# Earlier first Gram copies, earlier key loads, and a solve of the inverses with paired neighbours

## The chip, the cores and the metric

The kernel runs on one core of a Trainium2 chip. The metric is the device time of one execution in microseconds (us): 745.49 is the median of three runs of the kernel before, which lie between 743.66 and 747.66. The engines are named as in the profile: PE multiplies matrices (PEld is its loading of weights), DVE is the vector engine, ACT the scalar engine, POOL the general engine, SP the engine that issues most transfers.

## What is computed

Three layers stand one behind the other. The first is a linear attention with the delta rule, over 4 batches of 8 heads, 768 steps and vectors of 48. Its core in the reference:

```
k_n = k / (np.linalg.norm(k, axis=-1, keepdims=True) + 1e-06)
for t in range(S):
    kt, vt, bt = (k_n[:, :, t], v[:, :, t], beta[:, :, t, None])
    y[:, :, t] = np.einsum('bhd,bhde->bhe', q[:, :, t], state)
    v_old = np.einsum('bhde,bhd->bhe', state, kt)
    state = state + bt[:, :, :, None] * np.einsum('bhd,bhe->bhde', kt, vt - v_old)
```

The second takes the 4 x 768 x 384 output x through a product with w_in (384 x 1024), a gelu, a layer norm of one half, a mix over the 768 positions with w_sg, a gate and a product with w_out, and adds x. The third mixes each position with the one before it and forms sigmoid(xr w_r) * (relu(xk w_k)^2 w_v).

## The kernel before

The 768 steps are cut into 12 chunks of 64, two chunks to a group. Within a chunk the recurrence is replaced by a triangular system. For each group g, `gram(g)` lets PE form products of the keys: eight parts (4 parts i with 16 head pairs each in two halves), in blocks of 32 x 32, of which the diagonal blocks go to `GD` and the others to `GL`, by one ACT copy each (L342). `solver(g)` then inverts, on DVE, the 32 x 32 unit triangular matrices of all heads, 32 per partition: it transposes GD into `NT` (L360), forms the norms and c = beta / norm^2 (L364 to L380), scales the four 8 x 8 diagonal blocks of NT by c (L389), inverts the 8 x 8 blocks row by row in `Yt` (i = 1 to 7; each row is a product L355 and a reduce L393), copies the result to `Dm` and `NT` (L401, L403), and joins 8 x 8 blocks to 16 x 16 and to 32 x 32, again with products and reduces that all go through one buffer `tmp`. The last step transposes Dm into `DT` (L440). From the second group on, `couple(g, k)` multiplies GL and DT on PE (L456) to carry one 32-block into the next.

A prelude forms the first group: keys (kT0, kT1) are loaded, `gram(0)` runs in two sets, first the diagonal blocks (columns 0 to 32, four copies, `diag[:4]`), later the others (`diag[4:]`), then the first products of the scan and `gram(1)`. Meanwhile the weights of w_in are loaded and rounded into two parts each by a chain of ACT (L164), four DVE operations (L169 to L175), POOL (L177), ACT (L120) and POOL (L123). `early(n, t)` moves such background work on by n steps of t us.

Then 12 chunks are scanned in two halves of heads. `st_rq`, `st_d`, `st_n`, `st_s` and `st_y` are PE products with ACT copies between them (r at L473, the keys' products at L513, u at L526, the state at L540 and L555). `tick` brings in the background work, the solver of the next group and the Gram products of the one after that. The units of the second layer that are ready fill PE's stream in between. From some 300 us on PE works on the layers two and three alone.

The program order on PE, ACT, DVE and POOL is the order of the Python statements (`manual_schedule`), so what an engine does next is fixed by what was written first, and each engine waits in that order. A list `streams` holds running generators such as the solver; the background step lets each of them issue what its `yield` costs allow.

The order of SP's queue matters in the prelude: beta is written first in the program, then the keys, the weights of w_in, the queries and the tokens.

Of the kernel before, what the change touches and what calls it, by code (L numbers as in the profile page):

```python
# [7 lines left out]
F32 = mybir.dt.float32  # L8
# [3 lines left out]
AF = mybir.ActivationFunctionType  # L12
# [20 lines left out]
LOW0 = 1  # L33
WARM = 4
SV = 60
B0 = 1.0
PRE = 0.8
GRAM0 = 7
# [35 lines left out]
def vw(t, off, dims):  # L74

    a = t[:]
    return bass.AP(a.tensor, a.offset + off, [list(a.ap[0])] + [list(d) for d in dims])
# [9 lines left out]
def fused_kernel(  # L87
# [143 lines left out]
    def slot(tag, shape, dtype=F32):  # L231
        return wq.tile(shape, dtype, name="s" + tag, tag=tag)
# [16 lines left out]
    with ExitStack() as at:  # L249
# [13 lines left out]
        def load_k(s):  # L263
            if s >= 12:
                return
            kT[s] = kTb[s % NKT]
            nc.sync.dma_start(out=kT[s], in_=kt_d[s])

        def load_tok(s):
            t = ap2.tile([P, 2, NPR, D], F32, name="vk")  # L270
            vt[s], kt[s] = t[:, 0], t[:, 1]
            for h in range(2):
                nc.sync.dma_start(out=t[64 * h:64 * h + 64, 0], in_=vk[64 - 64 * h:128 - 64 * h, s, 0])
            nc.sync.dma_start(out=t[:, 1], in_=vk[:, s, 1])
# [3 lines left out]
                r = 64 * (1 - h)  # L278
                nc.sync.dma_start(out=SQ[o][s % 2][h][r:r + D, :, D:], in_=q_d[s, o, h])

        beta_sb = ap1.tile([P, NG, 32], F32, name="beta_sb")
        for h in range(2):
            nc.sync.dma_start(out=beta_sb[64 * h:64 * h + 64], in_=beta[64 - 64 * h:128 - 64 * h])

        banks = [ps2]

        def bank():
# [1 line left out]

        Sps = [ps1.tile([P, 8, D], F32, name=f"sps{o}") for o in range(2)]  # L290
        warm = ap1.tile([P, P], mybir.dt.bfloat16, name="warm")
        load_k(0)
        load_k(1)
        NT, GD, Dm = (slot(x, [P, 32, 32]) for x in G0[:3])
        tmp = slot(G0[3], [P, 1024])
        GLb = [slot(G0[4], [P, NU, 32]), slot(W0[2], [P, NU, 32]),
# [51 lines left out]
        Yt = ap1.tile([P, 16, 16], F32, name="Yt")  # L348
        GDs, GLs, DTs, neTs, joined = {}, {}, {}, {}, set()

        def product(a_off, a_dims, a_t, b_off, b_dims, b_t):

            sh = [d[1] for d in a_dims]
            tv = vw(tmp, 0, [(sh[1] * sh[2], sh[0]), (sh[2], sh[1]), (1, sh[2])])
            V.tensor_tensor(tv, vw(a_t, a_off, a_dims), vw(b_t, b_off, b_dims), op=ALU.mult)  # L355
            return tv, sh[0] * sh[1] * sh[2] / 960 + 0.16

        def solver(g):

            V.transpose(out=NT, in_=GDs[g])  # L360
            G.memset(Yt, 0.0)
            yield 1.14
            ss = ap1.tile([P, 32], F32, name="ss")
            V.tensor_scalar(ss, vw(NT, 0, [(33, 32)]), -1.0, 1e-36, op0=ALU.mult, op1=ALU.max)  # L364
            yield 0.2
            ne = yield from rsqrt(ap1, ss, 32, "rn")
            V.tensor_tensor(ne, ne, ss, op=ALU.mult)
            yield 0.2
            V.tensor_scalar(ne, ne, EPS, None, op0=ALU.add)
            yield 0.2  # L370
            neT = ap2.tile([P, 32], F32, name="neT")
            V.transpose(out=neT, in_=ne)
            neTs[g] = neT
            rn = ap1.tile([P, 32], F32, name="rn")
            V.reciprocal(rn, ne)
            yield 0.4
            V.tensor_tensor(rn, rn, rn, op=ALU.mult)
            yield 0.2
            c = ap1.tile([P, 32], F32, name="c")
            V.tensor_tensor(c, rn, beta_sb[:, g], op=ALU.mult)  # L380
            yield 0.2

            V.tensor_copy(vw(Yt, 0, [(64, 4), (9, 8)]), c.rearrange("p (m i) -> p m i", m=4))
            yield 0.1
            for m in range(4):
                blk = NT[:, 8 * m:8 * m + 8, 8 * m:8 * m + 8]
                V.tensor_tensor(blk, blk, vw(c, 8 * m, [(1, 8), (0, 8)]), op=ALU.mult)  # L389
                yield 0.15  # L390

            def total(o_ap, tv, t):
                V.tensor_reduce(out=o_ap, in_=tv, axis=AX.X, op=ALU.add)  # L393
                return t

            for i in range(1, 8):
                tv, t = product(32 * i, [(264, 4), (0, i), (1, i)], NT,
                                0, [(64, 4), (8, i), (1, i)], Yt)
                yield t
                yield total(vw(Yt, i, [(64, 4), (8, i)]), tv, t)  # L400
            V.tensor_copy(vw(Dm, 0, [(264, 4), (32, 8), (1, 8)]), vw(Yt, 0, [(64, 4), (1, 8), (8, 8)]))  # L401
            yield 0.4
            V.tensor_copy(vw(NT, 16, [(264, 2), (32, 8), (1, 8)]), vw(Yt, 0, [(64, 2), (8, 8), (1, 8)]))  # L403
            yield 0.3
            for dst in (0, 1):
                for p in range(2):
                    o = 16 * p
                    if dst == 0:
                        tv, t = product(32 * (o + 8) + o, [(32, 8), (0, 8), (1, 8)], NT,
                                        128 * p, [(0, 8), (8, 8), (1, 8)], Yt)  # L410
                        ov = vw(NT, 8 + 528 * p, [(1, 8), (32, 8)])
                    else:
                        tv, t = product(33 * (o + 8), [(32, 8), (0, 8), (1, 8)], Dm,
                                        8 + 528 * p, [(0, 8), (32, 8), (1, 8)], NT)
                        ov = vw(Dm, 32 * (o + 8) + o, [(32, 8), (1, 8)])
                    yield t
                    yield total(ov, tv, t)
                    if dst and p == 0:
                        V.tensor_copy(vw(NT, 24, [(1, 8), (32, 8)]), ov)
                        yield 0.2  # L420
            for last in (0, 1):
                if last == 0:
                    ops = [(vw(Yt, 16 * j, [(1, 16), (16, 4)]),
                            (32 * 16 + j, [(32, 16), (0, 4), (1, 16 - j)], NT,
                             16 + 33 * j, [(0, 16), (32, 4), (1, 16 - j)], NT))
                           for j in (12, 8, 4, 0)]
                else:
                    ops = [(vw(Dm, 32 * (16 + i), [(32, 4), (1, 16)]),
                            (32 * (16 + i) + 16, [(32, 4), (0, 16), (1, i + 4)], Dm,
                             0, [(0, 4), (16, 16), (1, i + 4)], Yt)) for i in (0, 4, 8, 12)]  # L430
                for i, (ov, args) in enumerate(ops):
                    tv, t = product(*args)
                    yield t
                    if g == 0 and last and i == 1:
                        V.memset(warm, 0.0)
                    if g == 0 and last and i == 2:
                        scale_v(0)
                    yield total(ov, tv, t)
            DT = DTb[g % 2]
            V.transpose(out=DT.rearrange("p u i -> p i u"), in_=Dm)  # L440
            DTs[g] = DT
            yield 1.14
            if g:
                p = point[0] + LAGC
                p += -p % 6 if p % 6 > 2 else 0
                for k in range(2):
                    later.append((p + 6 * k, lambda k=k: couple(g, k)))
# [16 lines left out]
        def scale_v(s):  # L464
            G.tensor_tensor(vt[s], vt[s], vw(neTs[s // 2], NPR * (s % 2), [(1, NPR), (0, D)]),
                            op=ALU.mult)
# [319 lines left out]
        for o in range(2):  # L786
            load_q(0, o)
        load_tok(0)
        diag = gram(0, ((0, 32), (32, 64)))
        for job in diag[:4]:  # L790
            for _, f in job:
                f()
            early(1, NPRE)
        streams.append([point[0], solver(0), "solve"])
        for s in range(2, NKT):
            load_k(s)
# [38 lines left out]
        def tick():  # L835
            g, n = divmod(point[0], 24)
            point[1] = min(g, 1) + 1
            gg, nn = divmod(point[0] - GRAM0, 24)
            if nn == 0 and 0 <= gg and gg + 2 < NG:
                grams.extend(gram(gg + 2))  # L840
            if n == 0 and g + 1 < NG:
                streams.append([point[0] + SOLVE0, solver(g + 1), "solve"])
            late = point[0] >= LATE
            if point[0] < LASTP and jobs and len(running) < RUN[1 + late] and n % (2 if late else EVERY) == 0:
                start_job(LJ5 if late else LJ)
            background(BUDGET * (B0 if g == 0 else 1))
            while len(jobs) > n_rest and len(running) < RUN[0]:
                start_job()
            if grams and (point[0] - GRAM0) % GSTEP == 0:
                for _, f in grams.pop(0):  # L850
                    f()
                used[0] += 1.1
                dense[0] += 1
            point[0] += 1
# [398 lines left out]
```

## Time and profile before

| what | value |
|---|---|
| median of 3 runs | 745.49 us (743.66 to 747.66) |
| profiled execution | 746.13 us |
| its span | 744.3 us |
| PE busy | 689.7 us (93%) |
| DVE busy | 506.3 us (68%) |
| ACT busy | 364.8 us (49%) |
| POOL busy | 202.5 us (27%) |

The span goes from the first to the last instruction that the profile holds. Busy time is time in which an engine executes; a wait of an instruction is idle time of its engine, and the trace puts down what released it. PEclk is the clock of PE that was granted, 1.00 for the higher level and 0.50 for the lower.

### The profile page before, as it was taken

The numbers are of one execution on the slowest core, as the hardware profiler recorded it, in microseconds if no ns is written. First come the engines' busy times: TensorE is split into PE (matmuls) and PEld (weight loads), VectorE is DVE, ScalarE is ACT, GpSimd is POOL, SyncE is SP. The second block draws the span as 40 slices with busy tenths as digits, with TensorE's granted clock in tenths as the row PEclk, the third lists the DMA queues.
The fourth block names the chain that finished last, engine by engine and source line by source line (L and its number), as shares of the span: only waits on it lengthen the run. The fifth ranks groups of instructions, "written<-read, shape, count | busy, mean of one in ns | idle before, by whom it ended". The sixth has DMA issues, their size and how long they took to land.

```text
span 744.3 us, 24530 instructions
## 1 busy us (share of the span) xinstructions
PE 689.7 (93%) x10688; PEld 622.4 (84%) x10688; DVE 506.3 (68%) x1014; ACT 364.8 (49%) x696; POOL 202.5 (27%) x253
## 2 busy tenths in 40 slices
PE   3459789998998999899999999999999999999998
PEld 3337568887886987779999999998989899999997
DVE  5989999897888796642566857598656464736251
ACT  3226656776676676774331413146445453626140
POOL 3033544454345255463131515330000000000000
PEclk9968989999999899999999999999999999999999
DMA  8502443675556566848763545259000000000000
GB/s 237 133 29 86 126 102 94 165 215 160 138 178 165 148 182 172 231 144 226 245 222 106 168 153 168 85 193 232 23 21 22 22 21 22 11 33 11 32 11 33
DMA packets 81547, 88.72 MB, mean 119 GB/s; under 512 B 24704, under 2 KB 64320, under 8 KB 81440
## 3 DMA queue, kind: packets, MB, share of 16 engines
q1 hardware_dynamic: 76384, 77.72, 35.3%
q0 software_dynamic: 5056, 9.44, 4.8%
q8 instruction: 84, 1.38, 0.7%
q14 instruction: 23, 0.19, 0.1%
HBM read 56.60 MB, written 25.82 MB: 111 GB/s over the span
## 4 chain that ended last, share of the span: by engine, by line
PE 67%; DVE 20%; issue 4%; DMA 4%; POOL 2%; ACT 2%; SPq 0%; POOLq 0%; ACTq 0%; DVEq 0%
PE ms L151 34%; PE ms L960 11%; PE ms L687 5%; DVE sg L355 5%; PE ms L635 4%; DVE sg L393 3%; PE ms L563 2%; PE ms L456 2%; PE sps L549 2%; DVE Yt L393 2%; PE rk L521 1%; PE ms L333 1%; PE rk L534 1%; PE rk L498 1%; DMA raw<-in_w_k_dram 1%
## 5 line engine op out<-in xcount | busy, mean ns | idle before, releaser
L151 PE MATMUL ms<-wvh,sl 128*128 128x384 f32 x192 | 64.7, 337 | 0.5 <-DVE sl L123 0.5
L151 PE MATMUL ms<-wvh,sh 128*128 128x384 f32 x192 | 64.6, 337 | 0.1
L151 PE MATMUL ms<-wvl,sh 128*128 128x384 f32 x192 | 64.5, 336 | 0.0
L1059 ACT ACTIVATE gh<-w 128x384 fp32r<-128x384 f32 x32 | 16.8, 526 | 93.8 <-DVE w L1058 93.8
L177 POOL TENSOR_TENSOR na<-na,raw 128x256 int32<-128x256 int32 (+2 forms) x43 | 35.9, 835 | 96.2 <-ACT gh L1059 40.7
L151 PE MATMUL ms<-xm_hi,sw0h 128*128 128x512 f32 x144 | 56.1, 390 | 0.0
L151 PE MATMUL ms<-xm_hi,sw0l 128*128 128x512 f32 x144 | 56.1, 389 | 0.0
L151 PE MATMUL ms<-xm_lo,sw0h 128*128 128x512 f32 x144 | 56.0, 389 | 0.0
L123 DVE TENSOR_TENSOR sl<-sg,sh 128x512 fp32r<-128x512 f32 x48 | 33.2, 692 | 28.8 <-ACT sh L120 28.7
L960 PE MATMUL ms<-sw0h,g 128*128 128x384 f32 x192 | 50.2, 335 | 0.0
L960 PE MATMUL ms<-ws1h,g 128*128 128x384 f32 x192 | 49.9, 334 | 0.0
L120 ACT ACTIVATE sh<-sg 128x512 fp32r<-128x512 f32 x48 | 30.3, 631 | 34.0 <-DVE sg L1172 34.0
L1189 DVE TENSOR_TENSOR sg<-sg,ms 128x384 f32<-128x384 f32 x24 | 13.3, 553 | 49.3 <-PE ms L151 49.3
L355 DVE TENSOR_TENSOR sg<-sg,Yt 128x512 f32<-128x512 f32 (+10 forms) x78 | 45.6, 584 | 1.7
L514 POOL TENSOR_SCALAR_AFFINE_SELECT SQ<-SQ 64x512 f32<-64x512 f32 x36 | 27.9, 774 | 50.2 <-ACT SQ L513 49.0
L1171 ACT ACTIVATE sg<-ms 128x512 f32<-128x512 f32 x48 | 28.6, 595 | 26.1 <-PE ms L151 24.1
L1172 DVE TENSOR_TENSOR sg<-sg 128x512 f32<-128x512 f32 x48 | 33.2, 692 | 10.8 <-ACT sg L1171 10.8
L687 PE MATMUL ms<-xl,wiu_hi 128*128 128x256 f32 x144 | 39.5, 296 | 0.0
L687 PE MATMUL ms<-xh,wiu_hi 128*128 128x256 f32 x144 | 38.4, 289 | 0.8 <-issue 0.8
L687 PE MATMUL ms<-xh,wiu_lo 128*128 128x256 f32 x144 | 38.5, 290 | 0.0
L151 PEld LDWEIGHTS ms<-wvh,sl 128*128 128x128 f32 x192 | 36.1, 188 | 0.8 <-DVE sl L123 0.8
L393 DVE TENSOR_REDUCE sg<-sg 128x64 f32<-128x512 f32 (+3 forms) x48 | 35.9, 748 | 0.9
(246 smaller groups left out, 2155.5 us busy)
## 6 DMA issues: line engine op xcount, KB each, us to landing
u_d<-ug SPq DMA_DIRECT2D x24, 256.0 KB, 3.9
u<-u_d SPq DMA_DIRECT2D x16, 384.0 KB, 4.9
vn_d<-v SPq DMA_DIRECT2D x22, 256.0 KB, 3.3
vk<-in_vk_dram SPq DMA_DIRECT2D x24, 192.0 KB, 3.7
vk<-in_vk_dram SPq DMA_DIRECT2D x12, 384.0 KB, 4.5
out_dram<-sg SPq DMA_DIRECT2D x24, 192.0 KB, 1.9
kT<-in_kt_d_dram SPq DMA_DIRECT2D x8, 512.0 KB, 4.5
SQ<-in_q_d_dram SPq DMA_DIRECT2D x36, 96.0 KB, 3.6
```

The costliest lines, as they stand in the source:

```text
L120: A.activation(hi, src, AF.Copy)
L123: eng_lo.tensor_tensor(lo, src, hi.bitcast(F32), op=ALU.subtract)
L151: T.matmul(pt, lhsT=a, rhs=b, start=(i == 0), stop=(i == n - 1))
L177: G.tensor_tensor(a.bitcast(I32), a.bitcast(I32), w_lo.bitcast(I32), op=ALU.add)
L355: V.tensor_tensor(tv, vw(a_t, a_off, a_dims), vw(b_t, b_off, b_dims), op=ALU.mult)
L393: V.tensor_reduce(out=o_ap, in_=tv, axis=AX.X, op=ALU.add)
L514: G.affine_select(out=pt, in_=pt, pattern=[[0, 8], [1, C]], compare_op=ALU.is_gt, fill=0.0, base=0, channel_multiplier=-1)
L635: T.matmul(vstat[g, b], lhsT=a[:, c], rhs=w[:, c], start=first, stop=last)
L687: T.matmul(vstat["u"][:, 2 * P * d:2 * P * d + 2 * P], lhsT=w[:, c, ds_], rhs=a[:, c].rearrange("p b t -> p (b t)"), start=first, stop=last)
L960: T.matmul(pt[:, :DM], lhsT=v[:, ds_], rhs=w, start=(c == 0 and i == 0), stop=(c == 5 and i == 2))
L1171: A.activation(r, pt, AF.Relu)
L1172: V.tensor_tensor(r, r, r, op=ALU.mult)
```

## The change

1. The two beta loads move behind the loads of the tokens (`load_beta`).
2. A memset of `warm` stands first on DVE, and 95 tiny products on it (32 x 32 weights, 8 columns) stand first on PE.
3. All four diagonal Gram parts are issued before the background work takes a step (`early(4, NPRE)` behind the loop instead of `early(1, NPRE)` within it).
4. In the solver one multiply scales the four blocks; row 1 is one multiply instead of a product and a reduce; the two copies out of Yt go from DVE to ACT; from the second level on products and reduces of independent halves stand side by side, each with its own place in `tmp` (`at`).
5. The solver of the second group begins one step earlier (SOLVE0 for g = 0).

```diff
+        V.memset(warm, 0.0)
         load_k(0)
         load_k(1)
+        beta_sb = ap1.tile([P, NG, 32], F32, name="beta_sb")
+
+        def load_beta():
+            for h in range(2):
+                nc.sync.dma_start(out=beta_sb[64 * h:64 * h + 64], in_=beta[64 - 64 * h:128 - 64 * h])
+
+        o = bank()
+        for i in range(NLEAD):
+            b0 = 32 * (i % 4)
+            T.matmul(o[b0:b0 + 32, i // 4 % 8, 0:8], lhsT=warm[b0:b0 + 32, 0:32],
+                     rhs=warm[b0:b0 + 32, 0:8], start=True, stop=True)
...
-            for m in range(4):
-                blk = NT[:, 8 * m:8 * m + 8, 8 * m:8 * m + 8]
-                V.tensor_tensor(blk, blk, vw(c, 8 * m, [(1, 8), (0, 8)]), op=ALU.mult)
-                yield 0.15
+            blk = vw(NT, 0, [(264, 4), (32, 8), (1, 8)])
+            V.tensor_tensor(blk, blk, vw(c, 0, [(8, 4), (1, 8), (0, 8)]), op=ALU.mult)
+            yield 0.4
+            V.tensor_tensor(vw(Yt, 1, [(64, 4)]), vw(NT, 32, [(264, 4)]), vw(Yt, 0, [(64, 4)]),
+                            op=ALU.mult)
+            yield 0.15
...
-            for i in range(1, 8):
+            for i in range(2, 8):
...
-            V.tensor_copy(vw(Dm, 0, [(264, 4), (32, 8), (1, 8)]), vw(Yt, 0, [(64, 4), (1, 8), (8, 8)]))
-            yield 0.4
-            V.tensor_copy(vw(NT, 16, [(264, 2), (32, 8), (1, 8)]), vw(Yt, 0, [(64, 2), (8, 8), (1, 8)]))
-            yield 0.3
+            A.activation(vw(Dm, 0, [(264, 4), (32, 8), (1, 8)]), vw(Yt, 0, [(64, 4), (1, 8), (8, 8)]),
+                         AF.Copy)
+            A.activation(vw(NT, 16, [(264, 2), (32, 8), (1, 8)]), vw(Yt, 0, [(64, 2), (8, 8), (1, 8)]),
+                         AF.Copy)
+
+            def pairs(ops, hooks={}):
+
+                for k, (x, e) in enumerate(ops):
+                    ov, args, at = e
+                    if x == "*":
+                        tvs[at], t = product(*args, at=at)
+                        yield t
+                    else:
+                        yield total(ov, tvs[at], 0.16 + args[1][0][1] * args[1][1][1] * args[1][2][1] / 960)
+                    if k in hooks:
+                        hooks[k]()
...
+                yield from pairs([("*", es[0]), ("*", es[1]), ("+", es[0]), ("+", es[1])])
...
+                    yield from pairs([("*", a), ("+", a), ("*", b), ("*", d), ("+", b), ("*", c_),
+                                      ("+", d), ("+", c_)])
...
+                    yield from pairs([("*", c_), ("*", d), ("+", c_), ("*", b), ("+", d), ("+", b),
+                                      ("*", a), ("+", a)], hooks)
...
         load_tok(0)
+        load_beta()
         diag = gram(0, ((0, 32), (32, 64)))
         for job in diag[:4]:
             for _, f in job:
                 f()
-            early(1, NPRE)
+        early(4, NPRE)
...
-                streams.append([point[0] + SOLVE0, solver(g + 1), "solve"])
+                streams.append([point[0] + (SOLVE0 if g else 0), solver(g + 1), "solve"])
```

The order on ACT at the head of the program. `sg_109` (before) and `sg_204` (now) are GD, `raw` and `wiv_hi` belong to the rounding of w_in, `sg_112` and `sg_207` are GL. Before:

```order
L342 ACTIVATE sg_109<-ms 128x8x32 x2
L164 ACTIVATE raw<-raw 128x256 x2
L342 ACTIVATE sg_109<-ms 128x8x32
L120 ACTIVATE wiv_hi<-na 128x256 x2
L342 ACTIVATE sg_109<-ms 128x8x32
L342 ACTIVATE sg_112<-ms 128x256 x4
```

And now:

```order
L351 ACTIVATE sg_204<-ms 128x8x32 x4
L165 ACTIVATE raw<-raw 128x256 x2
L121 ACTIVATE wiv_hi<-na 128x256 x2
L351 ACTIVATE sg_207<-ms 128x256 x4
L165 ACTIVATE raw<-raw 128x256 x2
```

The third and fourth copy into GD now stand before the four operations of the rounding.

The order on ACT further on in the changed kernel, where the copies out of Yt now stand; the rows on `sg_204` and `sw0h_208` are the copies of the second group's Gram products.

```order
L351 ACTIVATE sg_204<-ms 128x8x32
L351 ACTIVATE sw0h_208<-ms 128x256
L351 ACTIVATE sg_204<-ms 128x8x32
L351 ACTIVATE sw0h_208<-ms 128x256
L412 ACTIVATE sg_205<-Yt 128x4x8x8
L414 ACTIVATE sg_203<-Yt 128x2x8x8
L121 ACTIVATE wiv_hi<-na 128x256 x2
L497 ACTIVATE r_831<-rk 128x384
```

L412 and L414, which were L401 and L403 on DVE, stand behind all of these copies (two more such pairs of rows stand ahead) and before the first r of the scan.

The order on DVE in the first solve behind the last reduce into Yt; `sg_108` and `sg_203` are NT, `sg_110` and `sg_205` Dm, `sg_111` and `sg_206` tmp, `na` the rounding of w_in. Before:

```order
L169 TENSOR_SCALAR na<-raw 128x256
L401 COPY sg_110<-Yt 128x4x8x8
L403 COPY sg_108<-Yt 128x2x8x8
L355 TENSOR_TENSOR sg_111<-sg_108,Yt 128x512
L393 TENSOR_REDUCE sg_108<-sg_111 128x8x8
L355 TENSOR_TENSOR sg_111<-sg_108,Yt 128x512
L393 TENSOR_REDUCE sg_108<-sg_111 128x8x8
L171 TENSOR_SCALAR na<-na 128x256
L355 TENSOR_TENSOR sg_111<-sg_110,sg_108 128x512
```

And now:

```order
L170 TENSOR_SCALAR na<-raw 128x256
L364 TENSOR_TENSOR sg_206<-sg_203,Yt 128x512 x2
L404 TENSOR_REDUCE sg_203<-sg_206 128x8x8 x2
L364 TENSOR_TENSOR sg_206<-sg_205,sg_203 128x512
L172 TENSOR_SCALAR na<-na 128x256
L364 TENSOR_TENSOR sg_206<-sg_205,sg_203 128x512
```

The two copies are gone, products and reduces stand in pairs, and the product that reads `sg_205` is the first that needs a moved copy.

## Rows read from the trace of the kernel before

**Rows 1.** The page's first section: busy time, share, instructions of each engine.

```profile
PE 689.7 (93%) x10688; PEld 622.4 (84%) x10688; DVE 506.3 (68%) x1014; ACT 364.8 (49%) x696; POOL 202.5 (27%) x253
```

**Rows 2.** Busy time by stretch (count), with the granted clock, DMA share, GB/s.

```profile
0.00:34.00 34.00, 15.08 (x834) 13.38 (x834) 24.57 (x72) 10.53 (x23) 8.82 (x18) 1.00 0.79 203
...
96.07:102.50 6.43, 6.43 (x164) 4.86 (x164) 5.99 (x19) 2.50 (x5) 3.40 (x5) 0.50 0.27 73
...
241.20:245.90 4.70, 4.68 (x75) 4.42 (x76) 4.33 (x20) 1.98 (x4) 0.70 (x1) 0.50 0.63 186
```

**Rows 3.** Waits of PE from 0 to 34 us: total, times, longest.

```profile
PE ms L335 <- issue: 13.0, 5, 4.8
PE ms L333 <- DMA kT<-in_kt_d_dram: 5.9, 1, 5.9
```

**Rows 4.** The page's DMA queues: packets, MB, share of 16 engines.

```profile
q8 instruction: 84, 1.38, 0.7%
```

**Rows 5.** Timeline of PE, where bursts begin: start, length, [idle before].

```profile
12.07 0.21 PE L335 MATMUL ms<-kT 64*32 64x32 f32 x1 [2.93 <-issue]
...
23.37 0.21 PE L335 MATMUL ms<-kT 64*32 64x32 f32 x1 [4.81 <-issue]
...
28.18 0.24 PE L335 MATMUL ms<-kT 64*32 64x64 f32 x1 [1.25 <-issue]
...
31.52 0.21 PE L335 MATMUL ms<-sw0h 64*32 64x64 f32 x1 [1.35 <-issue]
```

**Rows 6.** Timeline of SP's queue, its first issue.

```profile
0.80 1.23 SPq L283 DMA_DIRECT2D beta_sb<-in_beta_dram  x2
```

**Rows 7.** Timeline of ACT, last copy of the second Gram, and 63 us.

```profile
33.63 0.44 ACT L342 ACTIVATE sw0h<-ms 128x256 f32<-128x256 f32 x1
...
63.55 1.19 ACT L459 ACTIVATE sg<-ms 32x512 f32<-32x512 f32 x2
```

**Rows 8.** Timeline of DVE in the first solve.

```profile
15.77 1.25 DVE L360 STREAM_TRANSPOSE sg<-sg 128x1024 f32<-128x1024 f32 x1 [3.51 <-ACT sg L342]
...
26.73 0.36 DVE L393 TENSOR_REDUCE Yt<-sg 128x28 f32<-128x196 f32 x1
...
27.20 0.38 DVE L401 COPY sg<-Yt 128x256 f32<-128x256 f32 x1
27.50 0.22 DVE L403 COPY sg<-Yt 128x128 f32<-128x128 f32 x1
...
29.08 0.69 DVE L355 TENSOR_TENSOR sg<-sg,Yt 128x512 f32<-128x512 f32 x1
29.80 0.69 DVE L393 TENSOR_REDUCE sg<-sg 128x64 f32<-128x512 f32 x1
30.41 0.28 DVE L171 TENSOR_SCALAR na<-na 128x256 f32<-128x256 f32 x1
30.61 0.68 DVE L355 TENSOR_TENSOR sg<-sg,sg 128x512 f32<-128x512 f32 x1
...
47.74 1.96 DVE L440 STREAM_TRANSPOSE sw0l<-sg 128x1024 f32<-128x1024 f32 x1
```

**Rows 9.** Timeline of DVE in the second solve.

```profile
54.04 1.23 DVE L360 STREAM_TRANSPOSE sg<-sg 128x1024 f32<-128x1024 f32 x1
...
67.17 0.36 DVE L393 TENSOR_REDUCE Yt<-sg 128x28 f32<-128x196 f32 x1
...
94.01 1.92 DVE L440 STREAM_TRANSPOSE DT<-sg 128x1024 f32<-128x1024 f32 x1
```

**Rows 10.** Timeline of PE, last work before the second inverse is awaited.

```profile
90.33 1.04 PE L726 MATMUL ms<-warm 128*128 128x512 bf16 x4
```

**Rows 11.** Waits of PE from 90 to 300 us.

```profile
PE ms L456 <- DVE na L169: 4.7, 1, 4.7
PE ms L456 <- DVE sw0l L440: 3.8, 2, 3.6
PE ms L456 <- DVE DT L440: 2.5, 2, 1.6
```

## What the change is expected to do

> **What bounds the kernel now.** I read the page's busy table first, then the busy time by stretch, then what the matrix engine (PE) waits for in each stretch, and last the timelines of the engines it waits for. The profiled execution took 746.13 us, 744.3 of it span, so 1.8 lie around the span; that is 0.6 above the median of the runs shown (745.49), and I take the sum from the profiled execution and leave that 0.6 inside the range. PE is busy 93% of the span [rows 1], so all that can be gained are its idle pieces. Of the first 34 us PE works 15.08 [rows 2]. It waits 5.9 us for the first keys and then five times for nothing that the profile shows, 13.0 us together [rows 3]. PE has 2 x 10688 instructions [rows 1] and 84 packets came over the instruction queue, 1.38 MB [rows 4]: about 254 instructions and 16 KB a packet. The five bursts of PE (I show four starts) begin 4.8 to 5.6 us apart while the key and weight loads fill the DMA engines, 3.34 apart afterwards [rows 5], and hold 128 pairs of a weight load and a product each. So in the prelude PE runs at the pace of its instruction stream. The vector engine (DVE) waits 3.51 us in front of the first transpose at 15.77, for a copy of the scalar engine (ACT) [rows 8], and then runs the solve without a gap to the transpose that ends at 49.70; PE's scan starts behind that. In the scan PE waits for DVE again: 4.7 us for the second group's inverse (the wait that ends at 96.07), and 3.8 and 2.5 us, in two waits each, for later ones [rows 11].
>
> **Term A, the start of the scan.** Three edits bring the first transpose forward. The two loads of beta hold the first DMA queue for 1.23 us [rows 6]; behind the token loads they cost nothing, since beta is read only behind the first transpose. The first keys, awaited until 5.9 [rows 3], land at about 4.65. The 95 tiny products are 190 PE instructions that wait for nothing but a DVE memset; they move the places where PE's stream runs into the next block. The two copies move ahead of the roundings. In the kernel before, 191 + 256 instructions run without a stall, which is 223 pairs; the third and fourth copy of the Gram matrix come from the burst at 12.07. Now the leads fill the first block, copies 1 and 2 (64 pairs each) the second, copies 3 and 4 the third, which is asked for when PE reaches the second, between 3.5 and 4.65, and needs 4.4 to 4.9 from there (before: 7.2 to 12.07 is 4.9). The third block starts at 8.7, its last copy is done near 11.3, and DVE's rounding work (which ended at 15.77 - 3.51 = 12.26) ends near 11.0, its loads coming 1.27 earlier. The transpose starts at 11.3 (10.5 to 12.1) instead of 15.77: 4.5 earlier.
>
> That is not all gain. The first level of the solve ends at 26.73 + 0.36 = 27.09, which is 11.3 after the transpose [rows 8]; with one multiply for four and without one reduce 10.8, so at 22.1. The two copies (0.38 + 0.22 [rows 8]) now stand on ACT. Two products and two reduces do without them (four at 0.61 to 0.69, plus one rounding), so DVE comes to the first product that needs one at about 25.0. But on ACT both stand behind all eight copies of the second Gram matrix, of which the last runs at 33.63 to 34.07 [rows 7], because its PE work is in the last blocks of the stream. The 190 leads cost one block more before that work, the earlier keys start the stream earlier. From 8.7, three blocks at the mean of the starts 12.07 to 28.18, 5.37, give 24.8; one at 4.1 (mean of 4.81 and 3.34) 28.9; one at 3.34 32.2. The second Gram ends there: copies till 34.2, the moved copy at 34.6, and DVE goes on at 34.5 (31 to 36: blocks at 4.1 throughout, or at 5.65 until 26), against 30.61 before [rows 8]. The rest of the solve was 49.70 - 30.61 = 19.09; it is 18.2 with pairs, since an operation behind an independent neighbour starts 0.61 after it where a dependent one starts 0.72 later (29.80 to 30.41; 29.08 to 29.80) [rows 8], and some 9 change. Scan start: 34.5 + 18.2 = 52.7 against 49.70: **+2.9**. If ACT's queue holds nothing up, DVE goes on at 25 and the start is at 43: -6.8. The other end is +4.2. I take the value that the starts of the bursts give.
>
> [...]
>
> **Term B, the second inverse.** The second solve's transpose started at 54.04, 4.34 behind the first solve's end; now it stands right behind it (0.35), since the solve begins one step earlier. It ended at 94.01 + 1.92 = 95.93 [rows 9], 46.2 after the first one's end. It loses 4.0 of start and about 2.0 of DVE work: copies 0.6, three small multiplies 0.3, one reduce 0.2, nine pairs at 0.1. That gives 40.4. PE itself had reached its place at 90.33 + 1.04 = 91.37 [rows 10], 41.7 after the first inverse. I add 1 for ACT: in its order the moved copy waits for DVE's first level (before: ACT came to that place at 63.55, the level ended at 67.53 [rows 7, 9]; now both start 4 earlier on DVE, leaving about 1 to 1.9). PE then arrives at 42.7 and is the later one; the wait ended at 96.07, 46.4 after: **-3.7** (-4.7 with no ACT delay, -2 with all of it twice).
>
> **Term C, the later inverses.** The waits of 3.8 and 2.5 us are one of 3.6, one of 1.6, and two below 1. Each solve loses the same 2.0 of DVE work, with other work interleaved in the same order: the three small ones go (0.3 + 1.6 + 0.9), the large one has one solve operation of about 1.3 fewer ahead of it. **-4.1** (0 to -4.1; -6.4 if all goes).
>
> **Term D, the clock.** [...]
>
> **Term E, ACT in the scan.** In each of five groups two copies of 0.6 together, and the wait for their input, stand ahead of PE's evictions. For the second group it is priced in B; for the others **+1** (0 to +2).
>
> **Sum:** 746.1 + 2.9 - 3.7 - 4.1 - 3 + 1 = 739.2. I predict 739. The main case's own range is 734 to 744.
>
> [...]
>
> **Rivals.**
> 1. ACT's queue isn't the wait, or PE's stream flows: the second Gram finishes before 25 and A is -6.8: 746.1 - 6.8 - 3.7 - 4.1 - 3 + 1 = 729.5. For it: the moved copies need 0.6 us and ACT is idle most of the prelude. Against it: five stalls of 13.0 us, and the same PE order behind the leads. Chance 0.15.
> 2. The gains in the scan are swallowed: PE's chain between the inverses is paced by its own instruction stream and by ACT's evictions, so B is about -2, C -1 and D 0: 746.1 + 2.9 - 2 - 1 + 1 = 747.0, and with DVE going on 2 us sooner than I take it 745. For it: PE's own arrival at 91.37 lies only 4.7 ahead of the wait's end. Chance 0.20.
> 3. Slower: the two copies on ACT become what PE waits for. In each of the five later groups ACT stands before them until DVE has its first level, with the evictions of u and of the states behind. At 1.9 us a group (half of the 4.0 of the second group) that is +9.5 instead of +1, and D is lost, since PE stands again: 739.2 + 8.5 + 3 = 750.7. With D lost it decides from 0.9 us a group on (746.1 + 2.9 - 7.8 + 5 x 0.9 = 745.7). For it: ACT came to that place 4.0 ahead of DVE in the second group. Against: ACT is busy only 49% [rows 1], and DVE's solve is earlier as well. Chance 0.13.
>
> **How the numbers follow.** My forecast holds 0.52, the rivals 0.15, 0.20 and 0.13. What the runs of this kernel can tell from no change is 0.5%, 3.7 us: 741.8 to 749.2. Faster: 0.42 of my case (its upper end crosses the bound), all of rival 1, 0.04 of rival 2: 0.61. Same: 0.09, 0.14 and 0.03: 0.26. Slower: 0.01, 0.02 and 0.10: 0.13. The range of 730 to 749 leaves out some of rival 1 below and most of rival 3 above, 0.17 together.
>
> **What would show it.** The first transpose near 11.3 in place of 15.77; then DVE idle some 9 us near 25 to 34, released by ACT's copy, with the second Gram's copies ahead of it; the scan's first product some 3 us later than 51.7; no wait above 1 us in front of the second inverse's product, PE busy up to it; no stretch at 0.50 there. Wrong would be: no DVE wait near 25 (then rival 1), or waits of PE for ACT in each group (rival 3), or PE's stall before the second inverse still above 2 us.

## The result, and the profile after

The changed kernel takes 750.37 us (median of 9 runs, 745.79 to 755.67) against 745.33 for the kernel before (9 runs, 743.26 to 747.66): ratio 1.007, 95% interval 1.0048 to 1.0092. It is slower by 0.7%, where 739 was forecast; the time lies above the range. Ratios here and below leave out the few executions that ran in the slower state. The profiled execution has a span of 748.8 us against 744.3, 4.5 more. The rows below are of it, unless said otherwise.

DVE in the first solve, as [rows 8] (start, length, engine, line, operation, [idle before]):

```profile
10.23 1.24 DVE L369 STREAM_TRANSPOSE sg<-sg 128x1024 f32<-128x1024 f32 x1
...
23.73 1.27 DVE L404 TENSOR_REDUCE sg<-sg 128x64 f32<-128x512 f32 x2
36.89 0.69 DVE L364 TENSOR_TENSOR sg<-sg,sg 128x512 f32<-128x512 f32 x1 [11.88 <-ACT sg L412]
...
52.95 1.96 DVE L464 STREAM_TRANSPOSE sw0l<-sg 128x1024 f32<-128x1024 f32 x1
...
55.15 1.23 DVE L369 STREAM_TRANSPOSE sg<-sg 128x1024 f32<-128x1024 f32 x1
```

The transpose that began at 15.77 begins at 10.23, and 14.8 us later DVE has nothing to do for 11.88 us: it waits for the copy L412. What was won at the head is lost there twice over; the inverse is done at 54.91 instead of 49.70.

ACT, as [rows 7]:

```profile
9.12 0.62 ACT L351 ACTIVATE sg<-ms 128x256 f32<-128x256 f32 x1 [0.21 <-PE ms L344]
...
30.21 0.61 ACT L351 ACTIVATE sg<-ms 128x256 f32<-128x256 f32 x1 [10.71 <-PE ms L344]
...
35.89 0.42 ACT L351 ACTIVATE sw0h<-ms 128x256 f32<-128x256 f32 x1
36.21 0.65 ACT L412 ACTIVATE sg<-Yt 128x256 f32<-128x256 f32 x1
...
69.14 0.67 ACT L412 ACTIVATE sg<-Yt 128x256 f32<-128x256 f32 x1 [4.19 <-DVE Yt L404]
```

The copy's input was complete at 22.4 (the last reduce of the first level in the same timeline, 22.05 + 0.36). ACT was idle for 10.71 us of the time until 36.21 (from 19.5 to 30.21), but it stood at the second Gram's first copy, which waits for PE, and the copy of Yt is behind that in its order. In the second solve it is the other way round: at 69.14 ACT waits 4.19 us for DVE, and what PE needs from ACT stands behind.

PE, where its bursts begin, as [rows 5]:

```profile
16.49 0.26 PE L342 MATMUL ms<-kT 64*32 64x32 f32 x1 [3.72 <-issue]
...
29.96 0.22 PE L344 MATMUL ms<-kT 64*32 64x64 f32 x1 [3.43 <-issue]
...
34.21 0.24 PE L344 MATMUL ms<-sw0h 64*32 64x64 f32 x1 [0.64 <-issue]
```

The last two blocks begin 7.27 (from 22.69, in the same timeline) and 4.25 us after the ones before them.

Waits of PE from 100 to 300 us, as [rows 11]:

```profile
PE ms L480 <- DVE sw0l L464: 1.9, 1, 1.9
PE rk L545 <- issue: 1.7, 3, 1.2
PE rk L558 <- ACT u L550: 1.6, 1, 1.6
PE ms L587 <- issue: 1.4, 2, 0.9
PE ms L711 <- issue: 1.4, 1, 1.4
PE ms L344 <- issue: 0.7, 1, 0.7
PE ms L480 <- ACT sw0h L537: 0.7, 1, 0.7
PE ms L342 <- issue: 0.2, 1, 0.2
```

The same stretch of the first trace of before, beside the waits for inverses of [rows 11]:

```profile
PE ms L563 <- issue: 0.8, 1, 0.8
PE ms L687 <- issue: 0.8, 1, 0.8
PE ms L335 <- issue: 0.3, 1, 0.3
PE sps L549 <- issue: 0.3, 1, 0.3
```

The 6.3 us of waits for later inverses are 1.9, and the 4.7 before the second inverse are gone. New in this stretch are 2.3 us of waits for ACT; those for PE's own instructions ("issue") are 5.4 us against 2.2.

That "issue" means instruction blocks in the scan too can be read from the packets of the instruction queue q8 in the packed traces. From the scan's first product on, every wait put to "issue" in both traces of both kernels ends 1.2 to 1.8 us after such a packet has landed, with one exception (1.75 us at 71.31 in the changed kernel).

The stretches at the lower clock, as [rows 2] (us; busy time of PE, PEld, DVE, ACT, POOL; granted clock; DMA share; GB/s):

```profile
108.54:115.37 6.83, 6.83 (x147) 4.90 (x140) 6.38 (x20) 3.56 (x7) 3.74 (x4) 0.50 0.47 111
...
221.20:224.60 3.40, 3.40 (x51) 3.18 (x54) 3.37 (x6) 0.00 (x0) 2.27 (x2) 0.50 0.02 6
...
245.08:251.90 6.82, 6.82 (x140) 6.34 (x133) 6.44 (x24) 2.29 (x5) 3.00 (x5) 0.50 0.47 138
```

And in the kernel before:

```profile
95.70:102.52 6.82, 6.45 (x164) 4.91 (x164) 6.38 (x21) 2.50 (x5) 3.40 (x5) 0.50 0.27 72
...
194.68:198.10 3.42, 3.42 (x104) 2.98 (x103) 3.08 (x20) 1.12 (x4) 0.00 (x0) 0.50 0.69 211
...
239.06:245.90 6.84, 4.68 (x75) 4.42 (x76) 6.46 (x22) 2.40 (x5) 2.43 (x4) 0.50 0.70 182
```

There are three behind 100 us, 17.1 us together; before there were 12.8 (the end of the one that began at 95.7, 3.4 at 194.7, and 6.8 at 239.1). So from 100 to 300 us the lower level (0.50) holds for longer than before. From each scan's first product to the end it does not: 23.9 us against 27.0.

### The profile page after: what moved, and what is told of

It reads as the page before. It is cut to its first block, busy times and chain, and to the rows that moved or that the text cites. A ratio compares the mean times of both kernels' runs of the same rounds, so it can differ in the third digit from the quotient of the medians.

```text
span 748.8 us, 24715 instructions
## 1 busy us (share of the span) xinstructions
PE 694.2 (93%) x10783; PEld 626.7 (84%) x10783; DVE 497.4 (66%) x979; ACT 367.9 (49%) x708; POOL 197.9 (26%) x253
## 4 chain that ended last, share of the span: by engine, by line
PE 80%; DVE 9%; issue 5%; ACT 2%; DMA 2%; POOL 1%; SPq 0%; POOLq 0%; ACTq 0%; DVEq 0%
PE ms L152 34%; PE ms L985 11%; PE ms L711 8%; PE ms L659 7%; PE ms L587 3%; PE ms L342 3%; PE rk L545 2%; PE rk L558 2%; PE rk L522 2%; PE sps L573 2%; PE ms L480 2%; DVE sg L364 2%; PE ms L750 1%; PE qk L525 1%; DVE sg L404 1%
## 5 line engine op out<-in xcount | busy, mean ns | idle before, releaser
L364 DVE TENSOR_TENSOR sg<-sg,Yt 128x512 f32<-128x512 f32 (+4 forms) x72 | 45.1, 635 | 1.6
L711 PE MATMUL ms<-xh,wiu_hi 128*128 128x256 f32 x144 | 38.9, 293 | 1.4 <-issue 1.4
L711 PE MATMUL ms<-xl,wiu_hi 128*128 128x256 f32 x144 | 40.1, 300 | 0.0
L538 POOL TENSOR_SCALAR_AFFINE_SELECT SQ<-SQ 64x512 f32<-64x512 f32 x36 | 26.3, 730 | 50.6 <-ACT SQ L537 49.4
L711 PE MATMUL ms<-xh,wiu_lo 128*128 128x256 f32 x144 | 39.3, 295 | 0.0
L124 POOL TENSOR_TENSOR raw<-na,raw 128x256 fp32r<-128x256 f32 (+2 forms) x31 | 28.0, 904 | 32.1 <-ACT raw L121 28.7
```

Of the source, the lines that this page charges most:

```text
L124: eng_lo.tensor_tensor(lo, src, hi.bitcast(F32), op=ALU.subtract)
L538: G.affine_select(out=pt, in_=pt, pattern=[[0, 8], [1, C]], compare_op=ALU.is_gt, fill=0.0, base=0, channel_multiplier=-1)
L711: T.matmul(vstat["u"][:, 2 * P * d:2 * P * d + 2 * P], lhsT=w[:, c, ds_], rhs=a[:, c].rearrange("p b t -> p (b t)"), start=first, stop=last)
```

## The experiments

Two theories were held against each other. Q: the place of the two moved copies in ACT's order is the loss. F: PE's chain in the scan goes at its own pace, so what is won early is waited off later. Unless said otherwise each kernel is the changed one with the edit shown; comparisons are with the kernel before, run beside it; the diffs of e7 and e8 are shown against e2, that of e10 against e6.

**Copies back on the vector engine, all six solves (e1), the first alone (e2), the later five alone (e3).**

```diff
-            A.activation(vw(Dm, 0, ...), vw(Yt, 0, ...), AF.Copy)
-            A.activation(vw(NT, 16, ...), vw(Yt, 0, ...), AF.Copy)
+            V.tensor_copy(vw(Dm, 0, ...), vw(Yt, 0, ...))      # e1: always
+            V.tensor_copy(vw(NT, 16, ...), vw(Yt, 0, ...))     # e2: if g == 0, e3: if g > 0
```

> The changed kernel with the two copies out of Yt back on the vector engine in all six solves; nothing else is touched. Theory Q (the scalar engine's queue: the copies wait behind the second Gram's copies in the first solve, 11.9 us of vector idle, and hold the scalar engine 4.2 us in the second solve): the vector engine goes from its reduces at 25.0 on to the first product that needs a copy at about 25.7 in place of 36.9, the first inverse is there near 44 in place of 54.9, the scan starts near 46 in place of 56.9, no 4.2 us wait of the scalar engine near 65, and the time is 734 to 740. Rival F (the scan between the inverses goes at the pace of PE's instruction stream, so what is won early is waited off before the second inverse or later): the scan starts as early, but the time is 743 to 748.

> The changed kernel with the two copies back on the vector engine in the first solve alone; the later five keep them on the scalar engine. Theory Q: scan start near 46 as with all six, but the second solve's copies still hold the scalar engine for about 4 us in front of PE's evictions; 738 to 743, some 3 above the kernel with all six on the vector engine. Rival F: the same 743 to 748 as with all six.

> The changed kernel with the two copies back on the vector engine in the five later solves; the first keeps them on the scalar engine. Theory Q: the first solve waits its 11.9 us as in the changed kernel (scan start near 57), the scalar engine doesn't wait in the second solve; 745 to 748, 2 to 5 below the changed kernel. Rival F: 749 to 752, as the changed kernel.

Measured: e1 744.25 (ratio 0.9992, 0.9958 to 1.0026), e2 737.32 (0.9886, 0.9838 to 0.9934), e3 754.32 (1.011, 1.0064 to 1.0157). In e2 the first solve (DVE's timeline) runs on:

```profile
22.75 0.38 DVE L413 COPY sg<-Yt 128x256 f32<-128x256 f32 x1
23.05 0.22 DVE L415 COPY sg<-Yt 128x128 f32<-128x128 f32 x1
...
41.70 1.92 DVE L470 STREAM_TRANSPOSE sw0l<-sg 128x1024 f32<-128x1024 f32 x1
```

The inverse is done at 43.62, 11.3 earlier, for 0.6 us of copies; the time falls by 13.1. So Q holds for the first solve: that one place is more than the whole loss. For the later solves both theories and my third rival were wrong: with these copies on DVE the kernel is 7 us slower (e1 against e2, whose intervals lie apart). e3 points the same way, 4 us above the changed kernel, but there the two intervals overlap. PE's longest waits from 100 to 300 us in e1 point to the reason:

```profile
PE ms L480 <- DVE sw0l L464: 4.2, 2, 4.1
PE ms L344 <- issue: 2.3, 1, 2.3
PE ms L587 <- issue: 2.1, 2, 1.1
PE ms L480 <- DVE DT L464: 1.9, 1, 1.9
...
```

It waits 6.1 us for the later inverses, as much as the kernel before (6.3), though the paired neighbours are in; in e2 it is 1.8. From the scan's first product to the end, all waits for DVE are 8.0 us in e1 and 3.0 in e2. Of the change it is the two copies off DVE that shorten these waits to 1.9.

**The head of the change alone, on the kernel before (e4)**: leads, keys before beta, first Gram's copies in one piece; the old solver.

```diff
+        V.memset(warm, 0.0)
...
+        for i in range(NLEAD):
+            T.matmul(...)
...
+        load_beta()
...
-            early(1, NPRE)
+        early(4, NPRE)
```

> The kernel before with the head of the change alone: the 95 products on warm, the beta loads behind the tokens, the four first Gram copies in one piece; the solver is that of before. Theory Q: first transpose at 10.2 in place of 15.8, no wait within the first solve, its end near 44.2 in place of 49.7 and the scan 5 us earlier; 739 to 742. Rival F: scan start as early, but 743.5 to 746.5.

Measured: 747.16 (739.87 to 754.60 in 10 runs; ratio 1.000, 0.9965 to 1.0036). The transpose is at 10.48, the scan's first product at 47.76, 3.9 earlier than in the kernel before, and its span in this trace is 748.0: at the end of the execution nothing of that is left. Here F is right: with the old solver an earlier start is lost again. The waits for inverses don't explain it, since they are as long as before (6.3 us for the later ones, 4.2 before the second one). What is longer from the scan's first product on are the waits for instruction blocks (10.3 us against 5.5) and the time at the lower clock (31.2 against 27.0), in a single trace of an execution (749.8) that lies above the median.

**The leads cut to 31 (e5) and raised to 223 (e9).**

```diff
-NLEAD = 95
+NLEAD = 31      # e5; e9: 223
```

> The changed kernel with 31 leading products in place of 95; nothing else. Theory I (PE's prelude goes at the pace of its instruction blocks of 256): the stream is 128 PE instructions shorter ahead of the second Gram, whose last part so falls into the block before; its last copy comes 3 to 4 us earlier than 35.9, the vector engine goes on near 33.5 instead of 36.9, the scan starts 3 us earlier, and the time is 746 to 748.5. Rival L (the leads are too short to matter, the second Gram waits for its keys or for copies): vector engine and scan start within 1 us of the changed kernel's, 749.5 to 751.5.

> The changed kernel with 223 leading products instead of 95: 256 PE instructions more, one block of the instruction stream, which take PE about 1.2 us long before the keys are there. Theory I (PE's prelude goes at the pace of its instruction blocks): every later piece falls into the next block. The first Gram's fourth copy moves from 9.1 to 11 to 13, the second Gram's last copy from 35.9 to 38 to 40, the vector engine goes on at 39 to 41 in place of 36.9, and the time is 2 to 3 us longer. Rival L (the products of the Gram matrices wait for keys and banks, not for instructions): all of these within 1 us of the changed kernel's.

Measured: e5 746.13 (744.77 to 750.48; ratio 1.0024, 0.9995 to 1.0052), but by another way than expected: the second Gram's last copy ends at 38.65 (36.31 in the changed kernel). My count left out PE's other instructions (in the changed kernel's trace the block from 29.96 to 34.21 holds 256, one of them a semaphore event), so its last two products fell into the next block all the same, and PE was at the lower clock (0.50) from 10.7 to 38.0. DVE goes on at 39.23 and the scan's first product is at 59.20, 2.3 later than in the changed kernel, yet the time is not longer. Between I and L it decides nothing. e9: 753.33 in a single run, which lies within the scatter of the changed kernel (745.79 to 755.67); its scan's first product is at 59.64, 2.8 later than in the changed kernel. PE's bursts in it:

```profile
7.22 0.21 PE L342 MATMUL ms<-kT 64*32 64x32 f32 x1 [4.20 <-issue]
...
10.83 0.26 PE L342 MATMUL ms<-kT 64*32 64x32 f32 x1 [1.67 <-issue]
...
29.41 0.34 PE L522 MATMUL rk<-sw0h,kT 64*64 64x48 f32 x1 [5.91 <-issue]
...
37.01 0.24 PE L344 MATMUL ms<-sw0h 64*32 64x64 f32 x1 [1.44 <-issue]
```

The keys were there at 4.34 in the changed kernel, and the leads end at 3.02; still the first Gram begins at 7.22, with PE idle for 4.20. The packets of the instruction queue in this trace land at 5.75 and 9.35, 1.47 and 1.48 us ahead of the bursts at 7.22 and 10.83. The fourth first-Gram copy moves from 9.12 to 12.83, DVE goes on at 39.68 instead of 36.89. Theory I, that the blocks of instructions pace PE in the prelude, is borne out; L is not.

**Copies on ACT in all solves, but ahead of the second Gram's copies in the first (e6).**

```diff
             A.activation(vw(NT, 16, ...), vw(Yt, 0, ...), AF.Copy)
+            if g == 0:
+                copied.append(1)
...
-                rest += [lambda j=j: whole(j) for j in gram(1)]
+                second += [lambda j=j: whole(j) for j in gram(1)]
+            if copied and second:
+                rest += second
+                second.clear()
```

> The changed kernel with both copies on the scalar engine in all six solves, but in the first solve they stand ahead of the second Gram's eight copies in its order instead of behind them (the second Gram's jobs are brought in once the copies are issued; PE's order stays as it is). Theory Q (the queue position is the whole loss): the copies run as soon as the first level is there, near 22.5; the vector engine has no wait there, the scan starts within 1 us of the kernel that has the first solve's copies on the vector engine (46.4), and the time is 736 to 739 like that kernel's 737.3. Rival A (the copies themselves don't belong on the scalar engine in the first solve): over 742.

Measured: 737.28 (733.63 to 738.66; ratio 0.988, 0.984 to 0.992). ACT:

```profile
22.72 0.67 ACT L413 ACTIVATE sg<-Yt 128x256 f32<-128x256 f32 x1 [3.76 <-DVE Yt L405]
23.30 0.29 ACT L415 ACTIVATE sg<-Yt 128x128 f32<-128x128 f32 x1
29.93 0.64 ACT L351 ACTIVATE sg<-ms 128x256 f32<-128x256 f32 x1 [6.34 <-PE ms L344]
```

The same instructions on the same engines, in another order on one of them, take 13 us less. The scan's first product is at 45.06, 11.8 earlier than in the changed kernel; from there to the end the two traces take the same 691.9 us, so the earlier start is the whole gain between them. Q is shown for the first solve.

**Copies on DVE in the first three solves (e7); the second solve one step later again, on e2 (e8).**

```diff
-            if g == 0:
+            if g < 3:                                      # e7
...
-                streams.append([point[0] + (SOLVE0 if g else 0), solver(g + 1), "solve"])
+                streams.append([point[0] + SOLVE0, solver(g + 1), "solve"])     # e8
```

> The changed kernel with the two copies on the vector engine in the first three solves, where the scalar engine had to wait for the first level in the changed kernel (11.9 us of vector wait, then 4.2 and 2.8 us of scalar wait), and on the scalar engine in the last three, where it waited 0.2, 0 and 1.3. Theory W (those waits are the price, and the 0.6 us taken off the vector engine the gain): 734 to 737, below the 737.3 of the kernel that has them on the vector engine in the first solve alone. Rival V (what counts in the later groups is the vector engine's work, not the scalar engine's wait): 738 to 743, towards the 744.3 of the kernel with all six on the vector engine.

> The kernel with the first solve's copies on the vector engine (737.3), and the second solve begun one step later again, as in the kernel before. Theory B (the earlier second solve takes PE's wait before the second inverse away): the second transpose begins some 4 us after the first inverse instead of 0.2, PE waits again about 2 to 4 us for the second inverse, and the time is 739.5 to 742. Rival N (PE's own chain is as late): no such wait, 736.5 to 738.5.

Measured: e7 738.46 (ratio 0.9901, 0.9864 to 0.9937), e8 737.83 (733.79 to 742.66; ratio 0.9898, 0.9839 to 0.9957). Neither can be told from e2. So ACT's waits in the second and third solve cost no time that these runs see, and the gain of e7 over e1, whose intervals lie apart, is in the last three solves. In e8 the second transpose begins at 48.14, 4.35 after the first inverse, and PE waits 1.7 us before the second inverse (none in e2): the wait is B's. The time is N's, but the interval of its four runs also holds the 739.5 to 742 of B, so they don't decide between the two.

**The first r ahead of the roundings too, on e6 (e10).**

```diff
             neTs[g] = neT
+            if g == 0:
+                scale_v(0)
...
+                second.append(lambda: next(body, None))
```

> The kernel whose first solve's copies stand ahead of the second Gram's (737.3), and in the same way the copy of the first residual r, which the first product of the scan waits 4.6 us for, stands ahead of the two roundings of w_in in the scalar engine's order (the scaling of the first values is issued right behind the norms for that). Theory Q (places in the scalar engine's queue set the start): r is there long before the first inverse, the scan starts at the first inverse, near 43.5 to 44 in place of 45.2 to 45.6, and the time is 735 to 736. Rival F (the scan behind it is held by other things): the start moves by the same 1.8 us, the time by less than 0.5.

Measured: 737.77 (734.18 to 742.04; ratio 0.9889, 0.9848 to 0.993). The scan's first product is at 43.94, right at the inverse and 1.1 before e6's. The time is no better, but the interval is some 3 us to either side, so neither theory is excluded for this last microsecond.

**Second traces of the changed kernel (e11) and of the kernel before (e12).**

> The changed kernel once more, for a second trace. Theory R (the losses in the scan, PE waits for its own instructions and the stretches at the lower clock, fall on other places in each execution): start of the scan and waits in the solves as before within 0.5 us (vector wait 11.9, scalar wait 4.2, scan start 56.9), but the places and the sum of the instruction waits and of the slow stretches between 100 and 300 us differ by 2 us or more. Rival S (they belong to the kernel): the same places.

> The kernel before once more, for a second trace. Theory R: its waits for the inverses and the scan start (51.7) come again within 0.5 us, while instruction waits and slow stretches between 100 and 300 us change their places. Rival S: the same places as in the first trace (0.8, 0.8, 0.3 and 0.3 us of instruction waits; slow at 194.7 and 239.1).

Measured: spans of 751.0 and 744.5. PE's longest waits from 100 to 300 us in e11:

```profile
PE ms L587 <- issue: 2.6, 1, 2.6
PE ms L480 <- DVE sw0l L464: 1.9, 1, 1.9
PE ms L711 <- issue: 1.9, 1, 1.9
PE rk L558 <- ACT u L550: 1.6, 1, 1.6
PE ms L344 <- issue: 1.1, 1, 1.1
...
```

DVE's wait in the first solve comes again (11.62), so do 1.9 for the inverse, 1.6 for u and the instruction wait at L711 with a slow stretch behind it (221.2 and 222.8). The slow stretch at 108.5 does not, and a wait of 2.6 at L587 with one at 267.2 takes its place; ACT's wait in the second solve is 1.57 instead of 4.19. In e12 PE waits 4.4 us for instructions (2.2 in the first trace), 5.3 for later inverses (6.3), and the first transpose is at 14.58, 1.2 earlier. Its slow stretches come at nearly the old places (94.1, 193.0 and 240.8 against 95.7, 194.7 and 239.1). So R holds in part: most waits between engines and, in the kernel before, the slow stretches belong to the kernel; the waits for instructions vary by 2 us from one execution to the next in both kernels, and are higher in the changed one in both traces (5.4 and 7.3 us from 100 to 300 us).

## Why the prediction was wrong

The mechanism of term A was right and its size too small. Terms B to D failed as a sum: they count the waits for DVE that go as time that is won, and put PE's waits for its own instruction blocks behind the scan's start at no change. From the scan's first product to the end (us):

| | before | before, e12 | changed | changed, e11 |
|---|---|---|---|---|
| PE waits for DVE | 12.7 | 11.4 | 2.4 | 3.4 |
| PE waits for instructions | 5.5 | 7.7 | 12.5 | 14.5 |
| PE waits for ACT | 5.2 | 5.8 | 5.5 | 6.9 |
| PE busy | 667.9 | 667.9 | 669.2 | 667.8 |
| time at the lower clock | 27.0 | 23.9 | 23.9 | 20.5 |
| whole stretch | 692.6 | 694.1 | 691.9 | 693.9 |

The waits for DVE fell by 10.3, more than the 7.8 that B and C counted together; those for instructions rose by about 7 in both pairs of traces.

- **Term A** was forecast as +2.9 and is +5.2 at the scan's first product (51.69 to 56.86). The head came better than forecast (10.23 against 11.3), the tail as forecast (54.91 - 36.89 = 18.0 against 18.2). The step that was mis-sized is "one at 4.1 ... 28.9; one at 3.34 32.2": the two blocks took 7.27 and 4.25. I had put the end of the DMA load where it was in the kernel before (the DMA share is 0.91 from 22.69 to 29.96 and 0.26 from 29.96 to 34.21; before it was 0.07 from 28.18 to 31.52); with leads e9's blocks begin 7.84 apart in the same place (21.57 to 29.41) and e6's 6.72 (22.96 to 29.68). Such a block was in the trace of before as well, one place earlier: with the burst that [rows 5] leaves out, 16.62, the starts are 4.55, 6.75 and 4.81 apart, not 4.8 to 5.6. DVE went on at 36.89, outside the 31 to 36 given.
- **Term B**: the second solve took 40.25 from the first inverse to its own (40.4 forecast), and PE didn't wait for it. PE's first product there stands 2.50 behind the kernel before (98.57), 43.7 after the inverse where it was 46.4: -2.7 against -3.7. ACT's longer stand (4.19 us where I had 1 to 1.9) is not the reason: in e11 ACT waits 1.57 and the distance is 43.8, in e1 the copies are on DVE and it is 43.6. Why PE arrives no earlier stays open. Whether the earlier start of the solve brings time e8 leaves open.
- **Term C** was right in its size, 6.3 to 1.9, -4.4 against -4.1; the cause was half wrong. I credited 2.0 us per solve to copies, multiplies and pairs alike; e1 keeps the pairs and the multiplies and waits 6.1.
- **Term D** is where the failed sum shows most. Its 3 us, which the sums of rivals 1 and 3 use as well, were my estimate; no run shows that PE is granted 1.00 where it stands less. In the scan PE stood less for DVE (2.4 us against 12.7), not less for instructions (12.5 against 5.5). The stretch behind the second inverse did go, as forecast (1.00 from 91.5 to 108.5), but one of the same length came at 108.5, and the one at 239.1 came at 245.1. Over the whole scan the lower clock held 3.1 us less (3.4 between the second traces), worth about 1.6 as an estimate, with 0.50 taken as half the speed of 1.00, where -3 was counted; PE's busy time did not fall (+1.3 and -0.1). In all, from the scan's first product (5.2 late) to its end (4.5 late) the changed kernel wins 0.7 us on the one before, where B to E came to -9.8; in e11 it loses 1.3 there.
- **Term E** in my sum was +1; over the scan PE's waits for ACT rose by 0.3. Of the 2.3 us from 100 to 300 us, the 1.6 for u are not the moved copies' doing: e3 has the later copies on DVE and the same wait of 1.6.
- **Slips in the working.** 52.7 against 49.70 is +3.0 and not +2.9; 46.2 less 4.0 and 2.0 is 40.2 and not 40.4; ACT's delay taken twice gives -2.7 (at 1) or -0.9 (at 1.9) for B and not -2. None of them decides.
- **Rivals.** Rival 1 fell. What it describes, no wait in ACT's order, is e6, and there too the sum is short: 737.3 measured for 729.5, with A as priced (45.06 against 51.69 is -6.6 for -6.8), so the missing 8 us are B to E. Rival 2 comes nearest, by its condition: PE's chain went at the pace of its own instruction stream. Its total fits with A larger still (747.0 and 2.3 more for A is 749.3), but not its terms, since C alone was -4.4 where it had -1. Rival 3 fell: moving the copies back to DVE in the later solves makes the kernel slower (e1 against e2), not faster.
- **Blocks and pairs.** In the prelude of e9 256 more instructions delay the first Gram by 2.9 us (4.34 to 7.22), and PE stands 4.20 there. In the scan PE waits at few blocks: from 100 to 300 us it runs 10895 instructions in the changed kernel, some 43 blocks, and 8 waits are put to "issue". The pairs: two products of 0.69 end up as one row of 1.28 for two in the trace of e6 and of the changed kernel (where 0.72 + 0.69 would be 1.41), so the independent neighbour does start early; but no run here shows a time that this saves.

What stays open is why more instruction blocks come late in the scan of the changed kernel. The difference of 7 us came in both pairs of traces, but no experiment isolates its cause, and in the single traces of the variants the sum lies anywhere from 5.6 (e8) to 15.8 (e3).

## What to carry to other kernels

Before an operation is moved to an idle engine, read what stands ahead of it in that engine's order and when that is released: ACT was idle for 10.7 us and still the copy came 13.8 us late, and 0.6 us saved on DVE cost 11.9. A move and a place are two edits: with the place mended (e6, or e2 for the first solve alone) the same change is 1.2% faster than before instead of 0.7% slower. A sum of waits that go is an upper bound for the gain where the same engine has other waits close behind; ask of each what is late next. Here it was PE's own instructions. And read a total such as the time at the lower clock over the whole stretch that the change touches: from 100 to 300 us it rose by 4.3, over the whole scan it fell by 3.1.

## What the runs showed of the hardware

Tiny products at the head of PE's stream cost 9 to 10 ns each (95 in 0.91 us, 223 in 1.97) and still set when all that follows may run, as they shift the places of the instruction blocks: with 223 of them PE idled 4.20 us in front of keys that had landed by 4.34 in the changed kernel. PE went on 1.2 to 1.8 us after a packet of the instruction queue had landed, in the prelude of e9 as in the scans of both kernels. In one execution (e5) PE ran at 0.50 from 10.7 to 38.0 us, and still the second Gram's last copy ended only 2.3 us later than in the changed kernel: PE stood for 13.6 of these 27.3 us, in four waits that begin where a block of 254 or 256 instructions ends.
